# Values of the first chunk loaded ahead of the first weights, with shorter planned transfers, in a list-scheduled attention and mixture-of-experts kernel

## The chip, the cores and the metric

The kernel runs on one core of one Trainium2 chip. The metric is the device time of one execution in microseconds; a kernel's time is the median of its runs. All runs shown here are of the undisturbed ("fast") state. Engines are called PE (TensorE), ACT (ScalarE), DVE (VectorE), POOL (GpSimd) and SP (SyncE). PEld is PE's weight load.

## The reference

```python
# B, H, S, D = 4, 8, 768, 48: gated linear attention, one state per head
f = 1.0 / (1.0 + np.exp(-f_logit))
for t in range(S):
    state = f[:, :, t, :, None] * state + np.einsum('bhd,bhe->bhde', k[:, :, t], v[:, :, t])
    y[:, :, t] = np.einsum('bhd,bhde->bhe', q[:, :, t], state)
# x = y as (3072, 384); 4 experts of 384 -> 1024 -> 384, mixed by probabilities
p = domain_probs / (domain_probs.sum(-1, keepdims=True) + 1e-09)
for e in range(E):
    h = np.maximum(x @ w1[e], 0.0)
    out += p[:, e:e + 1] * (h @ w2[e])
```

## The kernel before

The sequence is cut into six chunks of 128 steps, with four batches each. Each step of the work (a load, an activation, a group of matmuls) is an `Op` with a cost on each engine that may run it, a priority and a lag until its result can be used. A planner places the ops on modelled engines. The instructions are then emitted in the planned order, and on the chip each engine runs its own in order. So a planned duration has no effect of its own on the chip. It decides which instruction stands before which.

```python
    def ready(self, o, e):
        t = 0.0
        for d in o.deps:
            if d.end is None:
                return None
            t = max(t, d.end + (d.lag + self.LATENCY if d.engine != e else 0.0 if e == "PE" else 0.05))
        return t
    ...
            for e in ("PE", "ACT", "DVE", "POOL", "DMA"):
                while free_at[e] <= now + 1e-9:
                    for o in left:            # sorted by priority: the first that is ready
```

Loads of q, k and f go out on SP's queue. Chunk 0's values, cast to bf16 on the way, and all expert weights go out on POOL's queue. An op on the modelled engine "DMA" stands for the transfer behind such an issue and emits nothing.

```python
    def add_load(c, nm, b, n, prio, deps=(), cost=None):
        op = P.add(f"ld {nm}{c}.{b}", {"DMA": cost or (1.05 if c else 1.1) * n}, ..., lag=2.0)
    v_gate, issued = [(0, "k", 1), (0, "k", 2)], []
    def add_v(b, prio):
        issued.append(P.add(f"v issue {b}", {"POOL": 0.8}, ..., -600 + b,
                            deps=issued[-1:] + ([ld[v_gate[b]]] if b < 2 else []), lag=1.2))
        ld[0, "v", b] = P.add(f"ld v0.{b}", {"DMA": 1.1}, lambda _: None, prio, deps=issued[-1:], lag=2.0)
    for i, x in enumerate("f0 k0 q0 f1 k1 q1 f2 f3 k2 q2 v0 k3 q3 v1 v2".split()):
        ...
    for i, (e, which, ks, cols) in enumerate(pieces):          # 11 weight pieces
        iss = P.add(f"w issue {i}", {"POOL": 0.8}, ..., -600 + 3 * i, deps=issued[-1:] + ...)
        op = P.add(f"w {i}", {"DMA": 2.05 if i < 6 else 4.4}, lambda _: None, ..., deps=[iss], lag=1.0)
        if i == 0:
            add_v(B - 1, -459.5)                               # v3 after the first weights
```

Weight pieces are numbered from 1 in this text. Pieces 1 and 2 are the halves of expert 0's first matrix, 3 and 4 those of expert 1's, 5 and 6 the halves of expert 0's second matrix; the other five are whole matrices. PE's part before the first expert matmul is padded with matmuls on a constant tile ("fillers", line L644 or L642), as many as the plan has gaps:

```python
    for o in done:
        if o.engine == "PE" and o.start <= first:
            o.pad, t = int((o.start - t) / (0.42 if t < 7.0 else 0.25)), o.end
```

L374 is the first expert matmul (x times w1, into h), L389 the second (h times w2, into o), L310 and L365 transposes, L325 the attention scores, L340 the scores times v, L301 the products of q and k with the gates, L246 weight issues, L233 value issues. An h group is three L374 matmuls, an o group four L389 (with piece 5 or with piece 6). In the views of waits, L385 is the relu of h on ACT, L396 the sum of o on DVE, L226 and L228 are copies.

Of the kernel before, what the change touches and what calls it, by code (L numbers as in the profile page):

```python
# [102 lines left out]
def kernel(  # L103
# [12 lines left out]
    B, H, S, D = q.shape  # L116
# [23 lines left out]
    P = Plan(rooms)  # L140
# [90 lines left out]
    def load(c, nm, b, n):  # L231
        if (c, nm) == (0, "v"):
            ins[c, nm, b] = nc.gpsimd.dma_start(out=tl("vb", c, b), in_=srcs[nm][c, :, b * H:(b + n) * H, :])  # L233
            if b < 2:
                after(ins[c, nm, b], ins[v_gate[b]])
            return
        ins[c, nm, b] = nc.sync.dma_start(out=tl(nm, c, b // 2)[:, hh(b, n), :],  # L237
                                          in_=srcs[nm][c, :, b * H:(b + n) * H, :])
        if (c, nm, b) == (1, "f", 0):
            after(ins[c, nm, b], ins["w", 6])  # L240
        if (c, nm, b) == (1, "f", 1):
            after(ins[c, nm, b], ins["w", w_gate])
# [162 lines left out]


    ld = {}
    def add_load(c, nm, b, n, prio, deps=(), cost=None):
        op = P.add(f"ld {nm}{c}.{b}", {"DMA": cost or (1.05 if c else 1.1) * n}, lambda e: load(c, nm, b, n), prio,
                   deps=deps, takes=[(nm, c, b // 2)], lag=2.0)  # L410
        for i in range(n):
            ld[c, nm, b + i] = op
        return op


    v_gate, issued = [(0, "k", 1), (0, "k", 2)], []

    def add_v(b, prio):
        issued.append(P.add(f"v issue {b}", {"POOL": 0.8}, lambda _: load(0, "v", b, 1), -600 + b,
                            deps=issued[-1:] + ([ld[v_gate[b]]] if b < 2 else []), takes=[("vb", 0, b)], lag=1.2))  # L420
        ld[0, "v", b] = P.add(f"ld v0.{b}", {"DMA": 1.1}, lambda _: None, prio, deps=issued[-1:], lag=2.0)

    for i, x in enumerate("f0 k0 q0 f1 k1 q1 f2 f3 k2 q2 v0 k3 q3 v1 v2".split()):
        nm, b = x[0], int(x[1])
        if nm == "v":
            add_v(b, -1000 + i)
        else:
            add_load(0, nm, b, 1, -1000 + i)

    every = slice(0, None)  # L430
    pieces = [(e, 1, every, slice(i * F // 2, (i + 1) * F // 2)) for e in range(2) for i in range(2)]
# [2 lines left out]
    w_last, w_gate = len(pieces) - 1, len(pieces) - 3  # L434
    wd = {}
    for i, (e, which, ks, cols) in enumerate(pieces):
        if i == 7:
            add_load(1, "f", 0, 1, -454.5, deps=wd[2, 1], cost=0.1)
        if i == w_last:
            for x in ((1, "f", 1, 1), (1, "k", 0, 2), (1, "q", 0, 2), (1, "v", 0, 2)):  # L440
                add_load(*x, -430 + len(ld), deps=wd[3, 1])
        iss = P.add(f"w issue {i}", {"POOL": 0.8}, lambda _, i=i, x=(e, which, ks, cols): load_w(i, *x),
                    -600 + 3 * i, deps=issued[-1:] + ([ld[1, "k", 0]] if i == w_last else []))
        op = P.add(f"w {i}", {"DMA": 2.05 if i < 6 else 4.4}, lambda _: None, -400 if i == w_last else -460 + i, deps=[iss], lag=1.0)
        issued.append(iss)
        wd[e, which] = wd.get((e, which), []) + [op]
        if i == 0:
            add_v(B - 1, -459.5)
    for x in ((1, "f", 2, 2), (1, "k", 2, 2), (1, "q", 2, 2), (1, "v", 2, 2)):
        add_load(*x, -400 + len(ld), deps=wd[3, 1])  # L450

# [3 lines left out]
    def attention(c, slot, gran):  # L455
        G, X, Y, GS, ET, VB = {}, [], [], [], {}, {}
        more = c < C - 1
        for b0 in range(0, B, gran):
            p, d, half = slot(b0, 0) - 0.5, 0.43 if gran == 1 else 0.84, b0 // 2
            g1 = P.add(f"gate1 {c}.{b0}", {"ACT": d}, lambda e, b0=b0: gate1(c, b0, gran), p,  # L460
                       deps=[ld[c, "f", b0 + i] for i in range(gran)], takes=[("ex", c, b0)], frees=[("f", c, half)])
            g2 = P.add(f"gate2 {c}.{b0}", {"ACT": d}, lambda e, b0=b0: gate2(c, b0, gran), p + 0.1,
                       deps=[g1], takes=[("gp", c, half)], frees=[("ex", c, b0)])
            for b in range(b0, b0 + gran):
                G[b] = g2
        for b in range(B):
            s = lambda k: slot(b, k)
            half = b // 2
            pt_ = lambda kind, *x: ("ps_t", kind, c, b) + x
            on = lambda f, *x: (lambda e, b=b: f(c, b, *x))  # L470
            one = lambda f, *x: (lambda e, b=b: f(c, b, *x, e))
            cs = P.add(f"cs {c}.{b}", {"PE": 0.17 if c else 0.36}, on(pe_cs), s(0),
                       deps=[G[b]], takes=[pt_("cs")], lag=0.2, frees=[("gp", c, half)])
            ex = P.add(f"exps {c}.{b}", {"ACT": 0.98 if c else 0.82}, on(exps), s(0) + 0.1, deps=[cs],
                       takes=[("e", c, b)] + ([("egs", c, b)] if c == 0 else []), frees=[pt_("cs")])
            GS.append(P.add(f"egs {c}.{b}", {"POOL": 0.8}, on(dma_egs), s(10), deps=[ex], takes=[("egs", c, b)],
                            frees=[("e", c, b)], lag=2.8) if c and more else None)
            pe = {"DVE": 0.47} if c == 0 and b == B - 1 else {"DVE": 0.47, "POOL": 1.36} if c == 0 else None
            qm = P.add(f"q {c}.{b}", pe or ({"DVE": 0.8} if (c, b) < (1, 2) else {"POOL": 1.1}), one(product, 0), s(4) - 0.2,
                       deps=[ex, ld[c, "q", b]], takes=[("qk", c, b)], frees=[("q", c, half), ("e", c, b)])  # L480
            km = P.add(f"k {c}.{b}", pe or ({"DVE": 0.5} if (c, b) < (1, 2) else {"POOL": 1.0}), one(product, 1), s(4) - 0.1,
                       deps=[ex, ld[c, "k", b]], takes=[("qk", c, b)], frees=[("k", c, half), ("e", c, b)])
            vb = ld[0, "v", b] if c == 0 else P.add(f"v {c}.{b}", {"POOL": 0.5, "ACT": 0.52} if c == 1 else {"POOL": 0.5}, one(cast_v), s(4),
                       deps=[ld[c, "v", b]], takes=[("vb", c, b)], frees=[("v", c, half)])
            if (c, b) < (1, 2):
                tq = P.add(f"tpq {c}.{b}", {"PE": 0.22}, on(pe_tp, 0), s(4), deps=[qm],
                           takes=[pt_("tp")], frees=[("qk", c, b)], lag=0.2)
                tk = P.add(f"tpk {c}.{b}", {"PE": 0.22}, on(pe_tp, 1), s(4) + 0.01, deps=[km],
                           takes=[pt_("tp")], frees=[("qk", c, b)], lag=0.2)
                parts = [(slice(0, 2), [tq, tk])] if c or b < B - 1 else [(slice(j, j + 1), [tj]) for j, tj in enumerate((tq, tk))]  # L490
                et = [P.add(f"ev_tp {c}.{b}", {"DVE": 0.69, "ACT": 1.05} if c else {"DVE": 0.6, "ACT": 0.92} if len(parts) == 1 else {"DVE": 0.35, "ACT": 0.49},
                            lambda e, b=b, js=js: copy(e, tl("QK", c, b)[0:MP, js], tl("tp", c, b)[0:MP, js]), s(4) + 0.1,
                            deps=ds, takes=[("QK", c, b)], frees=[pt_("tp")]) for js, ds in parts]
            else:
                et = [P.add(f"tp {c}.{b}", {"DMA": 1.8}, on(dma_tp), s(4), deps=[qm, km], takes=[("QK", c, b)],
                            frees=[("qk", c, b)], lag=2.5)]
            ET[b], VB[b] = et, vb
# [181 lines left out]
```

## Time and profile before

| kernel before | value |
|---|---|
| time, median (range of the first 3 runs) | 298.62 us (298.36 to 298.94) |
| profiled span | 296.6 us |
| PE busy | 289.0 us, 97% |
| PE idle after the first expert matmul, by its waits | 0.6 us |
| first expert matmul starts | 19.75 us |
| weight pieces 1, 2, 5, 6 land at | 19.10, 21.98, 27.74, 29.75 us |

A line of a timeline is: start, duration, engine, line, operation, output<-inputs, shapes, count, and in brackets how long the engine was idle before it and what ended that.

### The profile page before, as it was taken

The page shows a single profiled execution, that of the slowest core. Times are in us where ns is not written, and L with a number is a line of the kernel's source. Part 1 is how long each engine was busy: PE and PEld are TensorE (multiplying, and loading weights), DVE is VectorE, ACT ScalarE, POOL GpSimd, SP SyncE. Part 2 cuts the span into 40 slices and gives each one's busy share as a digit, 9 for nine tenths or more (in the row PEclk, how much of TensorE's full clock was granted, in tenths as well). Part 3 has the DMA queues.
Part 4 walks back from the last instruction along what each step waited for, and adds up shares of the span by engine and source line. Part 5 has one row for each costly group of instructions (what it writes and reads, how often), then busy time and mean ns, then how long its engine had stood idle before and what let it go on. Part 6 is the DMA issues. An engine that isn't in the chain of part 4 may idle for free.

```text
span 296.6 us, 5591 instructions
## 1 busy us (share of the span) xinstructions
PE 289.0 (97%) x2172; PEld 170.0 (57%) x2172; DVE 126.1 (43%) x250; ACT 174.3 (59%) x317; POOL 106.1 (36%) x180
## 2 busy tenths in 40 slices
PE   6899999999999999999999999999999999999995
PEld 2476555567777775555555555555555555555553
DVE  6786012785763673045375235243523222101223
ACT  5656656666684667777477575554475544465440
POOL 5786401138767448144449372243220000000000
PEclk9999999999999999999999999999999999999999
DMA  7999999998979999998979932102432100200002
GB/s 157 200 169 206 207 192 210 189 210 167 201 152 166 191 171 185 209 187 164 198 133 218 179 60 35 27 0 67 122 61 30 27 2 27 80 2 0 0 2 106
DMA packets 136462, 36.43 MB, mean 123 GB/s; under 512 B 126812, under 2 KB 135644, under 8 KB 136436
## 3 DMA queue, kind: packets, MB, share of 16 engines
q1 hardware_dynamic: 125188, 29.35, 52.0%
q0 software_dynamic: 11248, 6.72, 16.4%
q8 instruction: 17, 0.28, 0.4%
q14 instruction: 9, 0.07, 0.1%
HBM read 31.51 MB, written 4.72 MB: 122 GB/s over the span
## 4 chain that ended last, share of the span: by engine, by line
PE 78%; DMA 14%; POOL 3%; SPq 2%; issue 1%; ACT 1%; DVE 0%; POOLq 0%
PE ps_m L389 37%; PE ps_m L374 35%; DMA w_sb<-in_moe_w_dram 10%; DMA k<-in_k_dram 4%; SPq L237 2%; POOL w_sb L246 2%; PE ps_t L325 2%; PE ps_t L340 1%; PE ps_t L336 1%; PE ps_t L273 1%; POOL vb L233 1%; PE ps_t L346 1%; ACT e L293 1%; DVE o L396 0%; ACT xT L226 0%
## 5 line engine op out<-in xcount | busy, mean ns | idle before, releaser
L385 ACT ACTIVATE h<-ps_m 128x512 bf16<-128x512 f32 (+2 forms) x188 | 102.4, 548 | 91.9 <-PE ps_m L374 88.9
L374 PE MATMUL ps_m<-xT,w_sb 128*128 128x512 bf16 (+3 forms) x708 | 152.8, 339 | 0.6 <-ACT xT L226 0.6
L389 PE MATMUL ps_m<-w_sb,h 128*128 128x384 bf16 (+1 forms) x776 | 152.6, 324 | 0.1
L389 PEld LDWEIGHTS <-h 128*128 128x128 bf16 x776 | 75.0, 98 | 59.0 <-DMA w_sb<-in_moe_w_dram 0.3
L396 DVE SCALAR_TENSOR_TENSOR o<-ps_m,pn,o 128x384 f32<-128x384 f32 (+1 forms) x73 | 44.5, 612 | 117.3 <-PE ps_m L389 111.1
L374 PEld LDWEIGHTS <-w_sb 128*128 128x128 bf16 x708 | 65.3, 98 | 43.5 <-issue 0.7
L301 POOL TENSOR_TENSOR qk<-q,e 128x384 bf16<-128x384 f32 x18 | 21.4, 1195 | 36.5 <-ACT e L293 34.3
L360 POOL TENSOR_TENSOR Sf<-Sf,egs 48x192 f32<-48x192 f32 x40 | 20.2, 504 | 36.5 <-DVE Sf L353 34.4
L329 DVE TENSOR_TENSOR AT<-ps_t,mask 128x512 bf16<-128x512 f32 x48 | 30.2, 683 | 5.1 <-PE ps_t L325 5.1
L383 DVE TENSOR_SCALAR h<-ps_m 128x256 bf16<-128x256 f32 (+2 forms) x40 | 19.3, 499 | 26.5 <-PE ps_m L374 13.1
L293 ACT ACTIVATE e<-ps_t 128x384 f32<-128x384 f32 x48 | 26.7, 668 | 5.0 <-PE ps_t L273 3.5
L301 POOL TENSOR_TENSOR qk<-k,e 128x384 bf16<-128x384 f32 x20 | 20.2, 1013 | 8.7 <-ACT e L293 5.5
L353 DVE TENSOR_TENSOR Sf<-Sf,ps_t 48x192 f32<-48x192 f32 x40 | 14.0, 350 | 10.3 <-PE ps_t L346 9.4
L246 POOL DMA_DIRECT2D w_sb<-in_moe_w_dram x11 | 8.8, 807 | 18.5 <-DMA k<-in_k_dram 17.2
L361 POOL CAST sb<-Sf 48x192 bf16<-48x192 f32 x40 | 13.6, 340 | 2.6
L398 ACT ACTIVATE o<-ps_m,pn 128x384 f32<-128x384 f32 x22 | 12.8, 582 | 2.5 <-PE ps_m L389 1.5
L644 PE MATMUL ps_m<-busy 128*128 128x512 bf16 x34 | 10.9, 423 | 1.5 <-DVE busy L144 1.5
L265 ACT ACTIVATE ex<-f 128x768 f32<-128x768 f32 (+1 forms) x14 | 10.4, 746 | 1.8 <-DMA f<-in_f_logit_dram 1.8
L298 POOL DMA_DIRECT2D egs<-e x16 | 9.0, 563 | 6.9 <-ACT e L293 6.9
L340 PE MATMUL ps_t<-vb,AT 128*128 128x48 bf16 x192 | 11.4, 184 | 0.0
L269 ACT ACTIVATE gp<-ex 128x768 bf16<-128x768 f32 (+1 forms) x14 | 10.5, 751 | 0.3
L340 PEld LDWEIGHTS <-AT 128*128 128x128 bf16 x192 | 9.9, 97 | 1.1
(54 smaller groups left out, 120.6 us busy)
## 6 DMA issues: line engine op xcount, KB each, us to landing
out_dram<-o SPq DMA_DIRECT2D x23, 192.0 KB, 2.0
w_sb<-in_moe_w_dram POOLq DMA_DIRECT2D x5, 768.0 KB, 18.0
k<-in_k_dram SPq DMA_DIRECT2D x10, 384.0 KB, 5.6
q<-in_q_dram SPq DMA_DIRECT2D x10, 384.0 KB, 5.5
v<-in_v_dram SPq DMA_DIRECT2D x10, 384.0 KB, 5.7
f<-in_f_logit_dram SPq DMA_DIRECT2D x9, 384.0 KB, 4.6
w_sb<-in_moe_w_dram POOLq DMA_DIRECT2D x6, 384.0 KB, 9.0
f<-in_f_logit_dram SPq DMA_DIRECT2D x6, 192.0 KB, 3.8
```

The lines of the kernel that those rows point to most:

```text
L246: ins["w", i] = nc.gpsimd.dma_start(out=w[:, e, ks, cols], in_=r[e][:, ks, cols])
L293: nc.scalar.activation(out=o, in_=i, func=AF.Exp, scale=1.0 if j else -1.0)
L301: engines[eng].tensor_tensor(out=tl("qk", c, b)[:, j, :, 0:D].rearrange("t (i r) d -> t i r d", r=2), in0=tl("qk"[j], c, b // 2)[:, hh(b), ...
L329: nc.vector.tensor_tensor(out=tl("AT", c, b)[:, r].rearrange("s i t -> s (i t)"), in0=tl("A", c, b, r).rearrange("s i t -> s (i t)"), in1= ...
L340: nc.tensor.matmul(out=y[:, h * D:(h + 1) * D], lhsT=AT[:, r, i, :], rhs=vb[:, h, :], start=(c == 0), stop=True, skip_group_check=True)
L353: nc.vector.tensor_tensor(out=Sf[rows, b], in0=Sf[rows, b], in1=KV[rows, :, r, :], op=ALU.add)
L360: nc.gpsimd.tensor_tensor(out=Sf[rows, b], in0=Sf[rows, b], in1=eg, op=ALU.mult)
L374: nc.tensor.matmul(out=hp(c, e, fc, n0, n1, nf)[:, f], lhsT=w1_sb[:, e, kk, (fc + f) * 128:(fc + f + 1) * 128], rhs=tl("xT", c)[:, kk, n0: ...
L383: nc.vector.tensor_relu(out=dst, in_=src)
L385: nc.scalar.activation(out=dst, in_=src, func=AF.Relu)
L389: nc.tensor.matmul(out=tl("op", c, e, nt, part)[:, cols], lhsT=tl("h", c, e, half_of(c, nt * T))[:, fc, nt * T:(nt + 1) * T], rhs=w2_sb[:, ...
L396: nc.vector.scalar_tensor_tensor(out=o, in0=op, scalar=pe, in1=o, op0=ALU.mult, op1=ALU.add)
```

## The change

Its intent is to have the values of all four batches earlier, to let POOL make products of q and k instead of running through weight issues, and to start PE's expert stream earlier by a plan with shorter transfers.

```diff
-        op = P.add(f"ld {nm}{c}.{b}", {"DMA": cost or (1.05 if c else 1.1) * n}, ..., lag=2.0)
+        op = P.add(f"ld {nm}{c}.{b}", {"DMA": cost or (1.05 if c else 1.1) * n}, ..., lag=lag)
-    v_gate, issued = [(0, "k", 1), (0, "k", 2)], []
+    v_gate, issued = [(0, "k", 1), (0, "f", 3)], []
-        issued.append(P.add(f"v issue {b}", {"POOL": 0.8}, ...
-        ld[0, "v", b] = P.add(f"ld v0.{b}", {"DMA": 1.1}, ..., lag=2.0)
+        issued.append(P.add(f"v issue {b}", {"POOL": 0.95}, ...
+        ld[0, "v", b] = P.add(f"ld v0.{b}", {"DMA": 0.87}, ..., lag=1.4)
-    for i, x in enumerate("f0 k0 q0 f1 k1 q1 f2 f3 k2 q2 v0 k3 q3 v1 v2".split()):
+    for i, x in enumerate("f0 k0 q0 f1 k1 q1 f2 f3 k2 v0 q2 v1 k3 v2 q3 v3".split()):
-            add_load(0, nm, b, 1, -1000 + i)
+            add_load(0, nm, b, 1, -1000 + i, cost=0.87, lag=1.5)
-                    -600 + 3 * i, deps=issued[-1:] + ...
-        op = P.add(f"w {i}", {"DMA": 2.05 if i < 6 else 4.4}, ..., lag=1.0)
+                    (-600 if i == 0 else -185) + 3 * i, deps=issued[-1:] + ...
+        op = P.add(f"w {i}", {"DMA": 1.95 if i < 6 else 4.2}, ..., lag=1.0)
-        if i == 0:
-            add_v(B - 1, -459.5)
-            ex = P.add(f"exps {c}.{b}", {"ACT": 0.98 if c else 0.82}, ...
+            ex = P.add(f"exps {c}.{b}", {"ACT": 0.98 if c else 0.95}, ...
-            pe = {"DVE": 0.47} if c == 0 and b == B - 1 else {"DVE": 0.47, "POOL": 1.36} if c == 0 else None
+            pe = {"DVE": 0.5, "POOL": 1.15} if c == 0 else None
```

More of the change, by code (lines that the diff above doesn't have):

```diff
@@ L407, with add_load @@
     ld = {}
-    def add_load(c, nm, b, n, prio, deps=(), cost=None):
+    def add_load(c, nm, b, n, prio, deps=(), cost=None, lag=2.0):
         op = P.add(f"ld {nm}{c}.{b}", {"DMA": cost or (1.05 if c else 1.1) * n}, lambda e: load(c, nm, b, n), prio,
-                   deps=deps, takes=[(nm, c, b // 2)], lag=2.0)
+                   deps=deps, takes=[(nm, c, b // 2)], lag=lag)
         for i in range(n):
@@ L413, in add_load @@
         return op
-    v_gate, issued = [(0, "k", 1), (0, "k", 2)], []
+    v_gate, issued = [(0, "k", 1), (0, "f", 3)], []
     def add_v(b, prio):
-        issued.append(P.add(f"v issue {b}", {"POOL": 0.8}, lambda _: load(0, "v", b, 1), -600 + b,
+        issued.append(P.add(f"v issue {b}", {"POOL": 0.95}, lambda _: load(0, "v", b, 1), -600 + b,
                             deps=issued[-1:] + ([ld[v_gate[b]]] if b < 2 else []), takes=[("vb", 0, b)], lag=1.2))
-        ld[0, "v", b] = P.add(f"ld v0.{b}", {"DMA": 1.1}, lambda _: None, prio, deps=issued[-1:], lag=2.0)
-    for i, x in enumerate("f0 k0 q0 f1 k1 q1 f2 f3 k2 q2 v0 k3 q3 v1 v2".split()):
+        ld[0, "v", b] = P.add(f"ld v0.{b}", {"DMA": 0.87}, lambda _: None, prio, deps=issued[-1:], lag=1.4)
+    for i, x in enumerate("f0 k0 q0 f1 k1 q1 f2 f3 k2 v0 q2 v1 k3 v2 q3 v3".split()):
         nm, b = x[0], int(x[1])
@@ L442 @@
         iss = P.add(f"w issue {i}", {"POOL": 0.8}, lambda _, i=i, x=(e, which, ks, cols): load_w(i, *x),
-                    -600 + 3 * i, deps=issued[-1:] + ([ld[1, "k", 0]] if i == w_last else []))
-        op = P.add(f"w {i}", {"DMA": 2.05 if i < 6 else 4.4}, lambda _: None, -400 if i == w_last else -460 + i, deps=[iss], lag=1.0)
+                    (-600 if i == 0 else -185) + 3 * i, deps=issued[-1:] + ([ld[1, "k", 0]] if i == w_last else []))
+        op = P.add(f"w {i}", {"DMA": 1.95 if i < 6 else 4.2}, lambda _: None, -400 if i == w_last else -460 + i, deps=[iss], lag=1.0)
         issued.append(iss)
         wd[e, which] = wd.get((e, which), []) + [op]
-        if i == 0:
-            add_v(B - 1, -459.5)
     for x in ((1, "f", 2, 2), (1, "k", 2, 2), (1, "q", 2, 2), (1, "v", 2, 2)):
@@ L473, in attention @@
                        deps=[G[b]], takes=[pt_("cs")], lag=0.2, frees=[("gp", c, half)])
-            ex = P.add(f"exps {c}.{b}", {"ACT": 0.98 if c else 0.82}, on(exps), s(0) + 0.1, deps=[cs],
+            ex = P.add(f"exps {c}.{b}", {"ACT": 0.98 if c else 0.95}, on(exps), s(0) + 0.1, deps=[cs],
                        takes=[("e", c, b)] + ([("egs", c, b)] if c == 0 else []), frees=[pt_("cs")])
```

## The prediction

> **What bounds the kernel now.** I first read the page's chain of waits and its slices, then TensorE's waits after the start-up, then the timelines of PE and POOL in the first 25 us, then the DMA's own record.
>
> From the page of the kernel before (busy tenths in 40 slices of 7.4 us, and the chain that ended last):
> ```profile
> PE   6899999999999999999999999999999999999995
> DMA  7999999998979999998979932102432100200002
> ...
> PE 78%; DMA 14%; POOL 3%; SPq 2%; issue 1%; ACT 1%; DVE 0%; POOLq 0%
> ```
> PE is full from the third slice to the last one: the kernel is a PE stream with a start-up before it. The DMA engines are full as well for about the first 60 us.
>
> The waits of PE, from 19.5 us to the end, have one entry only:
> ```profile
> PE ps_m L374 <- ACT xT L226: 0.6, 1, 0.6
> ```
> So after 19.5 us the PE stream has 0.6 us of holes. The time is (start of the first useful expert matmul) + (a fixed amount of PE work) + (holes) + (tail). A change in the start-up can win only what it moves that start, or lose what holes it opens.
>
> The PE timeline where the stream starts (start, duration, what):
> ```profile
> 19.11 0.81 PE L644 MATMUL ps_m<-busy 128*128 128x512 bf16 x3
> 19.75 0.82 PE L374 MATMUL ps_m<-xT,w_sb 128*128 128x256 bf16 x6
> ```
> L644 is filler that computes nothing; L374 is the first expert matmul. Its start has two conditions: xT of batches 0 and 1 (ACT's copy for batch 1 runs from 19.10 to 19.58) and the first weight piece, which is issued at 13.16 and takes 5.9 us to land (19.10). They are 0.5 us apart, so neither can be moved alone for a gain of more than that.
>
> The chain that ended last, in order of time, from 20 to 60 us:
> ```profile
> 20.53 21.10 DMA w_sb<-in_moe_w_dram
> ...
> 42.07 7.75 DMA k<-in_k_dram
> ...
> 50.37 8.82 DMA w_sb<-in_moe_w_dram
> 59.19 0.05 issue
> 59.24 0.82 PE ps_m L389 x4
> ```
> Up to 59.24 the chain is a stream of transfers, and PE takes the last weights 0.05 us after they land. So there are two bounds with almost no slack between them, PE's work and the DMA stream. A PE that starts earlier meets the same weights at the same time, unless the stream moves too.
>
> POOL's timeline, which orders the software DMA queue:
> ```profile
> 6.31 1.00 POOL L301 TENSOR_TENSOR qk<-k,e 128x384 bf16<-128x384 f32 x1 [2.43 <-ACT egs L295]
> 7.64 1.06 POOL L233 DMA_DIRECT2D vb<-in_v_dram  x1 [0.33 <-DMA k<-in_k_dram]
> 8.89 1.24 POOL L301 TENSOR_TENSOR qk<-k,e 128x384 bf16<-128x384 f32 x1 [0.19 <-ACT egs L295]
> 11.35 1.83 POOL L233 DMA_DIRECT2D vb<-in_v_dram  x2 [1.21 <-DMA k<-in_k_dram]
> 13.16 0.76 POOL L246 DMA_DIRECT2D w_sb<-in_moe_w_dram  x1
> 13.89 0.93 POOL L233 DMA_DIRECT2D vb<-in_v_dram  x1
> 14.81 5.51 POOL L246 DMA_DIRECT2D w_sb<-in_moe_w_dram  x7
> ```
> The values v1 and v2 wait for k2 (landed 11.05), v3 stands behind the first weights, and from 14.81 POOL does nothing but weight issues, so the products of batches 2 and 3 all fall to DVE.
>
> **What the Trainium skill says.** "DMA: Bandwidth & Descriptors", section "Queues, rings and completion order": each engine takes packets in turn from the queues that have work. The trace agrees: the q load that shared the engines with v0 landed 2.2 us after the load before it, against 0.9 us for loads alone. The same page, "Anatomy of one DMA": a software-queue transfer has about 2 us fixed besides its bytes; here the v issued at 11.35 first shows traffic in the queue in the 13 to 14 us window, which agrees. "SBUF — State Buffer", section "SBUF: two separate sides": a DVE instruction with two SBUF inputs and a GpSimd one that reads SBUF exclude each other. The trace fits: POOL's product took 1.24 us with a DVE product beside it for 0.4 us and 1.00 us with almost none. So POOL is a poor place for a product, but it is free of the PSUM work that DVE alone carries.
>
> **The change, part by part.** The program has a planner that lists instructions by priority on modelled engines; the diff changes its costs and order. What the chip then does is set by in-order queues. I worked the first 16 us of the new plan by hand from the costs in the code.
>
> 1. *v1 gated on f3 instead of k2.* f3 lands at 10.10, k2 at 11.05. POOL sat idle 1.21 us before v1, so v1, v2 are issued about 0.95 us earlier (10.4 and 11.35), v3 at 12.3 (13.89 before, 1.6 us earlier), and the first weights at 13.2 (13.16 before): one issue of 0.93 us comes in front of them and 0.95 us is won by the gate. The sum is about zero.
>
> 2. *v3 ahead of the first weights in the queue.* Its packets took about 0.8 us (the software queue moved 1264 packets in the 14 to 15 us window; a v has 128 x 8 = 1024). If the queue is saturated, the first weights land 0.8 us later, 19.9. But between 15 and 18 us the queue moved only 0.41 MB, against 0.2 MB per us later, so about 1 us is slack there; then they land near 19.1 as before. I take 19.0 to 20.0.
>
> 3. *Values move in among q2, k3, q3.* k3 and q3 share the engines with v1 and v2: estimated one to two transfers of 0.8 us later, q3 at 16.2 to 17.2 instead of 15.35.
>
> 4. *Weights 1 and later rank behind POOL's products.* In my hand plan DVE now does q1 and k1, and POOL does k2 and then q3 after the first weight issue. DVE loses two products (2 x 0.55 us) of batches 2 and 3 and gains k1. On the chip POOL then waits for q3: 16.2 to 17.2, plus 1.15 us, so weight issue 1 is at 17.4 to 18.4 instead of 14.81. The queue needs it by about 17 (first piece done near 18.5 to 19, less 2 us fixed). So the stream may starve by 0 to 1.5 us, less the slack that part 2 used: pieces 1 to 5 shift by -0.5 to +0.8 us.
>
> 5. *xT of batches 0 and 1.* In the old order y1 (17.45) stood behind transposes that waited for late copies. v1 lands about 1.4 us earlier and k1 is done 0.3 us earlier, so y1 could run near 15.9 and xT near 17.6. But in my plan the transposes of q3 stand before the transpose of batch 1; if POOL makes q3 at 17.4 to 18.4, xT comes at 18.5 to 19.6. Against 19.58, that is a gain of 0 to 1 us.
>
> 6. *Shorter planned loads.* These give fewer fillers (L644) and an earlier planned start (my plan: first weights at 18.1, while about 19.4 is to be expected). Fillers that vanish become idle, which costs nothing unless PE cools; it still has attention work in between.
>
> Sum: the start is max(xT 18.5 to 19.6, weights 19.0 to 20.0) plus 0.15 us, near 19.4, against 19.75: -0.35 us. The DMA stream to 59 us carries the same bytes and shifts by about -0.5 to +0.8. As both bounds count, I expect between -1 and +1 us, centre -0.4: 298.62 - 0.4 = 298.2 us.
>
> **Rivals.** *The DMA stream as the only bound:* the chain up to 59.24 speaks for it, and the full DMA slices; then the new start is worth nothing and a starved queue shows in full: 299 to 300 us. Against it: most pieces have some tenths of us of slack at their first use. *Start-up latency as the only bound, weights keeping up:* xT at 18.5, start at 18.7, about 297.5 us. For it: 0.5 us between the two conditions, and 15 to 18 us is badly used; against it: v3 before the weights. *A reshuffled plan:* an earlier planned start moves priorities for later chunks and can remove or add holes such as the 0.6 us one at 67.38; about 0.5 us either way. *PE cools:* a wait of 2 us or more before the first weights; half-rate matmuls cost perhaps 1 us. The mean clock of 0.998 speaks against it, and the attention matmuls go on.
>
> **Range and chances.** The outcomes lie between 296.8 (both bounds 1.5 us earlier, with the hole gone) and 300.0 (the queue starved and PE waiting). Two per cent is 6.0 us; the whole start-up before 19.75 us is the only thing touched, and a third of it would have to vanish, or a hole of that size to open behind it. I give 0.01 to faster, 0.975 to same, 0.015 to slower.
>
> **What would show it.** POOL's timeline: four v issues ahead of the first weight issue, at about 10.4, 11.4, 12.3 for v1 to v3, the first weights at about 13.2, then one or two products before the second weights at 17.4 to 18.4. PE's timeline: first L374 near 19.4, fewer L644. The landing of the first weights: 19.0 to 20.0. PE's waits after the start: whether a wait on weights appears between 22 and 60 us. I would be wrong if POOL did not stop for q3 (then the weights come earlier and the gain is over 1 us), or if the new plan left PE waiting on weights that it believed to be there 1.3 us earlier.

## More of the kernel before

```profile
24.90 3.44 PE L374 MATMUL ps_m<-xT,w_sb 128*128 128x128 bf16 x33
28.18 1.46 PE L389 MATMUL ps_m<-w_sb,h 128*128 128x384 bf16 x8
29.48 0.81 PE L374 MATMUL ps_m<-xT,w_sb 128*128 128x512 bf16 x3
30.13 1.46 PE L389 MATMUL ps_m<-w_sb,h 128*128 128x384 bf16 x8
```

There is no bracket, so PE waits for nothing. The first L389 needs piece 5 at 28.18 and has had it since 27.74, when it landed; piece 6 landed at 29.75.

## The result, and the profile after

The changed kernel took 301.26 us (300.86 to 301.63, 4 runs) against 298.49 us for the kernel before in the same rounds. The ratio is 1.0088, 95% interval 1.0070 to 1.0105. Ratios here are the mean time of one kernel's fast runs over that of the other's of the same rounds, so not quite the ratio of the quoted medians. A repeat (r3) gave 1.0115 (1.0094 to 1.0136). The change costs about 2.7 us, where I had predicted a gain of 0.4 us and no more than 300.0 us.

The page of the changed kernel, slices and chain:

```profile
PE   6979999999999999999999999999999999999995
DMA  8999999998979879996989632102331100200002
...
PE 83%; DMA 7%; SPq 3%; POOL 3%; issue 1%; DVE 1%; ACT 0%; POOLq 0%; DVEq 0%; ACTq 0%
```

At this scale nothing is to be seen: PE looks as full as before. POOL's timeline is as predicted, with the four value issues ahead of the first weights, then two products, then the second weight issue, 2.2 us later than before:

```profile
10.22 2.64 POOL L233 DMA_DIRECT2D vb<-in_v_dram  x3 [1.66 <-DMA f<-in_f_logit_dram]
12.83 0.77 POOL L246 DMA_DIRECT2D w_sb<-in_moe_w_dram  x1
13.59 1.39 POOL L301 TENSOR_TENSOR qk<-k,e 128x384 bf16<-128x384 f32 x1
16.08 0.99 POOL L301 TENSOR_TENSOR qk<-q,e 128x384 bf16<-128x384 f32 x1 [1.10 <-DMA q<-in_q_dram]
17.01 7.17 POOL L246 DMA_DIRECT2D w_sb<-in_moe_w_dram  x9
```

The first piece lands at 19.18 and PE's stream starts at 19.23, so the start-up is where I had put it. The difference is in PE's waits from 18 us to the end, of which the kernel before had one, of 0.6 us:

```profile
PE ps_m L389 <- DMA w_sb<-in_moe_w_dram: 1.4, 2, 1.2
PE ps_m L374 <- ACT h L385: 0.4, 1, 0.4
PE ps_t L365 <- ACT yb L226: 0.3, 1, 0.3
PE ps_m L389 <- DVE o L396: 0.2, 1, 0.2
```

(Columns: who waited <- for whom: us in total, times, the longest.) The two waits on weights lie here, to be read against the four lines of the kernel before:

```profile
24.64 3.13 PE L374 MATMUL ps_m<-xT,w_sb 128*128 128x384 bf16 x32
27.99 0.82 PE L389 MATMUL ps_m<-w_sb,h 128*128 128x384 bf16 x4 [0.22 <-DMA w_sb<-in_moe_w_dram]
28.65 0.81 PE L374 MATMUL ps_m<-xT,w_sb 128*128 128x512 bf16 x3
30.64 0.81 PE L389 MATMUL ps_m<-w_sb,h 128*128 128x384 bf16 x4 [1.18 <-DMA w_sb<-in_moe_w_dram]
```

Two things differ. The work between is shorter: one h group of expert 1 before the first L389, where the kernel before has three; then one o group, one h group and at once the o group that needs piece 6, where the kernel before has two o groups on each side (the counts of 8). And piece 6 lands at 30.60, not 29.75. The chain of waits of the changed kernel leads from there back to POOL's product:

```profile
10.09 5.85 DMA q<-in_q_dram
...
16.08 0.99 POOL qk L301
17.07 3.07 POOL w_sb L246 x4
20.14 10.45 DMA w_sb<-in_moe_w_dram
30.60 0.04 issue
30.64 0.81 PE ps_m L389 x4
```

The traffic between 18 and 20 us shows what the late issue did, before first and changed below (for all queues: packets, bytes, mean rate, and how many packets were small):

```profile
DMA packets 1171, 0.36 MB, mean 179 GB/s; under 512 B 921, under 2 KB 1170, under 8 KB 1170
```
```profile
DMA packets 158, 0.16 MB, mean 79 GB/s; under 512 B 3, under 2 KB 158, under 8 KB 158
```

The queue ran nearly dry. Summed from 8 us on, the changed kernel has moved 0.17 MB less by 30 us, which is 0.8 us at the stream's 0.21 MB per us.

**A ledger of PE.** Some matmul records are missing from each trace, but the weight loads are complete: 2168 in the trace of the kernel before and 2157 in that of the changed one, in the order of the program (the four float32 transposes of the probabilities left out). I took the distance from each weight load to the next and subtracted the streaming time of its matmul, columns / 2.4 + 2.5 ns. The Trainium skill, "TensorE: Matmul & The Clock Gate", section "Back-to-back issue gap", gives this formula for an isolated matmul, and for a stream with weight loads about 131 ns at 512 columns. The trace has 216 ns for 512 columns with their weight loads, so the formula is what fits here and the 131 ns is not. What is left, summed by stretch, is loss. The start of the stream is that of the first L374 weight load, 19.54 in the kernel before. As differences to the kernel before, in us:

| stretch | changed | e4 | n3 | s1 | s2 | s3 |
|---|---|---|---|---|---|---|
| start of the expert stream | -0.31 | +1.17 | +0.05 | +0.36 | +0.80 | +0.09 |
| attention work left after the start | +0.36 | +0.36 | 0 | 0 | 0 | 0 |
| loss, start to 26 us | +0.67 | +0.20 | -0.12 | -0.12 | 0 | 0 |
| loss, 26 to 35 us (pieces 5 and 6) | +1.74 | +1.28 | 0 | +1.40 | -0.05 | +2.56 |
| loss, 35 to 54 us | 0 | +0.10 | +0.05 | +0.10 | +0.21 | 0 |
| loss, 54 to 70 us | -0.95 | -1.00 | -1.00 | -1.00 | -1.11 | -0.95 |
| loss, 70 to 90 us | +1.22 | +0.06 | +0.04 | +0.15 | +0.18 | +0.06 |
| after 90 us, and the tail | -0.06 | -0.08 | 0 | +0.34 | 0 | -0.06 |
| sum = difference of the profiled spans | +2.67 | +2.10 | -0.98 | +1.23 | +0.01 | +1.70 |

(The other columns are experiments below, one profile each. Sums can be off by 0.02 from rounding.) The largest entry of the changed kernel is the 1.74 us at pieces 5 and 6.

### The profile page after: what moved, and what is told of

Read it like the earlier page. It is cut to its first block, busy times and chain, and to the rows that moved or that the text cites. A ratio compares the mean times of both kernels' runs of the same rounds, so it can differ in the third digit from the quotient of the medians.

```text
span 299.2 us, 5540 instructions
## 1 busy us (share of the span) xinstructions
PE 287.7 (96%) x2133; PEld 169.8 (57%) x2161; DVE 127.4 (43%) x249; ACT 172.3 (58%) x316; POOL 107.8 (36%) x182
## 4 chain that ended last, share of the span: by engine, by line
PE 83%; DMA 7%; SPq 3%; POOL 3%; issue 1%; DVE 1%; ACT 0%; POOLq 0%; DVEq 0%; ACTq 0%
PE ps_m L389 40%; PE ps_m L374 37%; DMA w_sb<-in_moe_w_dram 3%; SPq L237 3%; DMA q<-in_q_dram 2%; PE ps_t L325 2%; POOL qk L301 1%; DMA egs<-e 1%; PE ps_t L340 1%; PE ps_t L336 1%; POOL w_sb L246 1%; PE ps_t L273 1%; PE ps_t L346 1%; DVE o L396 1%; DVE Sf L353 0%
## 5 line engine op out<-in xcount | busy, mean ns | idle before, releaser
L389 PE MATMUL ps_m<-w_sb,h 128*128 128x384 bf16 (+1 forms) x776 | 153.6, 324 | 1.8 <-DMA w_sb<-in_moe_w_dram 1.4
L374 PE MATMUL ps_m<-xT,w_sb 128*128 128x512 bf16 (+3 forms) x682 | 152.2, 338 | 1.7 <-ACT h L385 0.4
L389 PEld LDWEIGHTS <-h 128*128 128x128 bf16 x776 | 74.7, 98 | 61.4 <-issue 1.8
L374 PEld LDWEIGHTS <-w_sb 128*128 128x128 bf16 x708 | 65.5, 98 | 42.9 <-issue 0.8
L329 DVE TENSOR_TENSOR AT<-ps_t,mask 128x512 bf16<-128x512 f32 x48 | 29.9, 683 | 8.4 <-PE ps_t L325 8.4
L301 POOL TENSOR_TENSOR qk<-q,e 128x384 bf16<-128x384 f32 x19 | 22.4, 1184 | 25.7 <-ACT e L293 16.4
L383 DVE TENSOR_SCALAR h<-ps_m 128x256 bf16<-128x256 f32 (+1 forms) x41 | 20.5, 514 | 17.1 <-PE ps_m L374 15.1
L228 POOL CAST vb<-v 128x384 bf16<-128x384 f32 x17 | 8.4, 516 | 16.7 <-DMA v<-in_v_dram 12.3
L269 ACT ACTIVATE gp<-ex 128x768 bf16<-128x768 f32 (+1 forms) x14 | 10.4, 749 | 0.3
L226 ACT CAST yb<-ps_t 128x384 bf16<-128x384 f32 (+1 forms) x16 | 7.5, 471 | 5.1 <-PE ps_t L340 5.1
```

What stands on the lines that cost most here:

```text
L301: engines[eng].tensor_tensor(out=tl("qk", c, b)[:, j, :, 0:D].rearrange("t (i r) d -> t i r d", r=2), in0=tl("qk"[j], c, b // 2)[:, hh(b), ...
L329: nc.vector.tensor_tensor(out=tl("AT", c, b)[:, r].rearrange("s i t -> s (i t)"), in0=tl("A", c, b, r).rearrange("s i t -> s (i t)"), in1= ...
L374: nc.tensor.matmul(out=hp(c, e, fc, n0, n1, nf)[:, f], lhsT=w1_sb[:, e, kk, (fc + f) * 128:(fc + f + 1) * 128], rhs=tl("xT", c)[:, kk, n0: ...
L383: nc.vector.tensor_relu(out=dst, in_=src)
L389: nc.tensor.matmul(out=tl("op", c, e, nt, part)[:, cols], lhsT=tl("h", c, e, half_of(c, nt * T))[:, fc, nt * T:(nt + 1) * T], rhs=w2_sb[:, ...
```

## The experiments

**Theory B, the plan's order.** The planner's own dates for the landings of pieces 5 and 6 are 30.05 and 32.10 in the kernel before, which is 2.3 us later than they came (27.74, 29.75). In the changed kernel they are 25.87 and 27.82, which is 2.1 and 2.8 us earlier than they came (27.94, 30.60). The plan therefore puts the o groups too early, and an in-order PE stands before them with h groups behind that could run. **Theory A, the starved queue.** Products on POOL ahead of the second weight issue let the queue run dry, so all later pieces are late. **Rivals**: the values ahead of the weights, the new ranking of weight issues, or TensorE's clock.

Each call of runs shared one chip and the runs of the kernel before; calls went to different chips, so I compare ratios across calls.

### First call: one part undone, or one part alone

e1, the ranking of weight issues undone in the changed kernel:

```diff
-                    (-600 if i == 0 else -185) + 3 * i, ...
+                    -600 + 3 * i, ...
```

> The changed kernel with one part undone: weight issues rank ahead of POOL's products again, so the second weight issue follows the first product on POOL (about 15.0 us instead of 17.0). Theory A, the starved queue: in the changed kernel the stream moved 0.16 MB between 18 and 20 us against 0.36 MB before and stays 0.15 MB (0.75 us) behind; if the issue is earlier, the sixth weight piece lands near 29.8 instead of 30.6 and PE's wait for it (1.2 us) shrinks to about 0.4: about 300.2 us, and 299 if the starvation accounts for all of the loss. Theory B, the plan's order: the planner still believes that pieces 5 and 6 land at 25.9 and 27.8, so PE still asks for them too early: waits of 0.8 to 1.5 us stay, 300.5 to 301.3 us.

Measured: 301.01 us, ratio 1.0074 (1.0050 to 1.0097). Pieces now land earlier (21.50 for piece 2, 29.20 for piece 6), and no wait on pieces 5 and 6 is left in its profile. But the time hardly moved: the expert stream started at 20.57 us instead of 19.23. The mean clock, 0.994 in this profile, does not explain it: the four runs at 0.993 and 0.994 took 299.95 to 301.43 us, the two at 0.998 and 1.000 took 300.19 and 301.38.

e2, the planned landing of the weights 2 us later in the changed kernel:

```diff
-        op = P.add(f"w {i}", {"DMA": 1.95 if i < 6 else 4.2}, ..., lag=1.0)
+        op = P.add(f"w {i}", {"DMA": 1.95 if i < 6 else 4.2}, ..., lag=3.0)
```

> The changed kernel with one number changed: the planner believes that each weight piece lands 2 us later (planned landing of pieces 5 and 6: 27.9 and 29.8; seen in the changed kernel: 27.9 and 30.6). POOL's order is the same, so the queue starves as before. Theory B, the plan's order: PE's waits on the weights between 26 and 35 us (1.7 us lost) fall under 0.5 us: 299.3 to 300.0 us. Theory A, the starved queue: the weights are as late as before and PE only waits elsewhere: 301.0 to 301.4 us.

Measured: 299.55 us (299.11 to 301.55), ratio 1.0050 (1.0022 to 1.0078). e3, both edits:

> Both edits at once. If starved queue and plan's order each carry part of the loss: 298.3 to 299.2 us, the waits on weights gone and the sixth piece near 29.8. If a third cause carries it (the 1.2 us lost between 70 and 90 us, or the late attention of batches 2 and 3): 299.5 us or more with the waits gone.

Measured: 299.19 us (298.01 to 301.21), ratio 1.0026 (0.9993 to 1.0060).

The runs of e2 and e3 fall apart by their mean granted clock. In e2, four runs with 0.994 to 1.000 took 299.11 to 299.57 us and two with 0.989 took 301.10 and 301.55. In e3, three with 0.999 or more took 298.01 to 298.36, two with 0.994 took 300.03 and 300.17, and one with 0.989 took 301.21. The page's clock row in the changed kernel and in e2 (tenths, 40 slices):

```profile
PEclk9999999999999999999999999999999999999999
```
```profile
PEclk9969999999999999999999999999999999999999
```

And the fillers, two in the changed kernel, then four in e2:

```profile
18.18 0.59 PE L642 MATMUL ps_m<-busy 128*128 128x512 bf16 x2
```
```profile
21.82 1.88 PE L642 MATMUL ps_m<-busy 128*128 128x512 bf16 x4
```

In e2 they follow one another at 0.4 us, in the changed kernel at 0.22. The Trainium skill, "TensorE: Matmul & The Clock Gate", section "What's actually happening", has a gate that halves the clock after an idle window of some 3.4 us, and calls the window free-running. That agrees with the factor of two, and with runs of one kernel falling either way; no run here shows the window itself. So these experiments mix two things, and I read the runs that kept their clock: 299.1 to 299.6 for e2, 298.0 to 298.4 for e3. They were chosen after the fact, and not by one bound (a run at 0.994 counts in e2 and not in e3), so this is a hint and not a measurement of the two edits.

e4, the kernel before with only the planned transfers (0.87 and lags 1.5 and 1.4 for loads and values, 1.95 and 4.2 for weights, 0.95 for a value issue):

> The kernel before with nothing but the shorter planned transfers (loads 0.87, weights 1.95 and 4.2 us); values and priorities as before, weights issued one after another. Theory B, the plan's order: pieces 5 and 6 are planned at 26.8 and 28.8 and come near 27.8 and 29.8, so waits on weights appear that the kernel before does not have: 299.5 to 300.5 us. Theory A, the starved queue: no starvation here, so 298.0 to 298.7 us as before.

Measured: 300.02 us, ratio 1.0046 (1.0025 to 1.0068), where Theory B had it, in part by luck: by the ledger 1.28 us of the loss is at pieces 5 and 6, but 1.17 us is a later start, which no theory had. The waits on weights that the kernel before does not have appear with the planned numbers alone:

```profile
PE ps_m L389 <- DMA w_sb<-in_moe_w_dram: 0.9, 2, 0.7
PE ps_m L374 <- DVE xT L228: 0.5, 1, 0.5
```

It is not quite free of Theory A: the new plan also moved a product ahead of the first weight issue, which came at 14.52 instead of 13.16, so piece 1 landed at 20.67 and piece 6 at 31.85.

The new ranking on top of the kernel before needs no run: the orders of instructions on all engines come out the same as without it.

### Second call: the same with the clock held up

To take the clock out I added 14 fillers in the start-up to the changed kernel, e1, e2 and e3 alike:

```diff
-            o.pad, t = int((o.start - t) / (0.42 if t < 7.0 else 0.25)), o.end
+            o.pad, t = int((o.start - t) / (0.42 if t < 7.0 else 0.25)) + WARM.get(o.name, 0), o.end
+WARM = {"cs 0.0": 2, "y 0.1": 2, "tpk 0.3": 3, "tpq 0.3": 3, "xt 0.1": 2, "at 0.3": 2}
```

> The changed kernel with 14 more fillers in the start-up, so that TensorE's clock does not drop (some runs of the last experiments had filler spacing of 0.43 us between 17 and 23 us, twice the 0.22 of a warm clock, and were 1 to 3 us longer). The changed kernel itself had no such dip after 10 us, so nothing should change: 300.9 to 301.5 us, first expert matmul at 19.2 to 19.6, waits on weights as in the changed kernel. If the late warm-up (10 us instead of 5) were the cause of the loss: 299 us.

Measured: 301.59 us, ratio 1.0098 (1.0064 to 1.0132). One of its six runs had a lower clock (0.994, 304.07 us).

> The same fillers, and weight issues ranked ahead of POOL's products again. Without the clock dips of its first version this shows the starved queue alone: the second piece is issued near 15.0, pieces land 0.7 to 1.4 us earlier (sixth near 29.2), and the wait on them shrinks by about as much. Theory A: 299.7 to 300.4 us. If only the plan's order counts: 300.9 to 301.4 us.

Measured: 301.98 us, ratio 1.0088 (1.0057 to 1.0119), a miss. Its waits on pieces 5 and 6 are gone, but the ledger finds the losses of 70 to 90 us as in the changed kernel and a new hole of 1.4 us that ends at 116.5 us, where PE waits for a gate of ACT.

> The same fillers, and the planner told that weights land 2 us later; POOL's order as in the changed kernel. Theory B: like the undisturbed runs of its first version (299.1 to 299.6 us), now in all runs, with the waits on weights between 26 and 35 us gone and the loss between 70 and 90 us gone too. If the gain of those runs had another origin: above 300.5 us.

Measured: 299.57 us (299.33 to 300.60), ratio 1.0014 (0.9988 to 1.0040).

> The same fillers and both edits. If the two causes add up and the clock explains the spread of its first version (298.0 to 301.2 us): 298.0 to 298.5 us in all runs, mean clock 0.998 or more. If the clock has nothing to do with the spread, it stays 298 to 301.

Measured: 300.26 us (299.39 to 300.40), ratio 1.0032 (1.0006 to 1.0057), with clocks of 0.998 or more; the expected time was missed by 1 to 2 us.

The fillers did their work on the clock: the mean clock of 23 of the 24 runs is 0.998 or more. They did not bring the first warm-up forward (w1's fillers at 8.7 us still follow one another at 0.4 us, as the changed kernel's do), so the late warm-up that w1's expectation names was not tested; the changed kernel's stream starts early in spite of it. But the stream of w3 and w4 started at 22.2 and 22.5 us. How much of that the fillers did and how much the weights that were planned later is not told apart; with the fillers alone (w1) it started at 20.25. What stands is w3 against w1: the same order on POOL, the weights planned 2 us later, and 0.8% less time. Undoing the ranking alone (e1, w2) did not repair anything in either form.

### Third call: the values' order alone, and other plans

n1, the kernel before with only the new order of the values (gate, list, and v3 ahead of the first weights):

> The kernel before with the values' order alone (v1 gated on f3, v3 ahead of the first weights, values in among q2, k3, q3), old planned costs, old priorities. Weight issues follow one another right after v3, so the queue does not starve; the plan stays pessimistic (pieces 5 and 6 planned at 30.05 and 32.1, expected near 27.5 and 29.5), so no waits on weights. If the shorter planned loads are what costs 2.7 us: 298.0 to 299.2 us. If the values ahead of the weights are what costs: 300.5 to 301.5 us, with the first weights landing late.

Measured: 297.85 us, ratio 0.9970 (0.9952 to 0.9989). The values ahead of the weights are not the cause; they help.

n2, the changed kernel with the planned transfers put back:

```diff
-            add_load(0, nm, b, 1, -1000 + i, cost=0.87, lag=1.5)
+            add_load(0, nm, b, 1, -1000 + i)
-        ld[0, "v", b] = P.add(..., {"DMA": 0.87}, ..., lag=1.4)
+        ld[0, "v", b] = P.add(..., {"DMA": 1.1}, ..., lag=2.0)
-        op = P.add(f"w {i}", {"DMA": 1.95 if i < 6 else 4.2}, ...
+        op = P.add(f"w {i}", {"DMA": 2.05 if i < 6 else 4.4}, ...
```

> The changed kernel with the planned transfers (loads, values, weights) put back to the old durations and lags; order of values, new ranking of weight issues and new costs of products stay. The plan then puts no product ahead of the second weight issue, the same with the old ranking, so the ranking does nothing. If the planned durations are the cause, through both the early order and the products in front of the weight issue: 298.0 to 299.2 us, no waits on weights. If the ranking or the new product costs are the cause: above 300.5.

Measured: 298.38 us, ratio 0.9984 (0.9967 to 1.0002). With the old durations the whole loss is gone, although ranking and product costs are those of the change. The planned durations are the cause.

n3, the changed kernel with planned transfers near the measured ones, and the old ranking (with these durations the new ranking gives the same instructions in the same order):

```diff
-            add_load(0, nm, b, 1, -1000 + i, cost=0.87, lag=1.5)
+            add_load(0, nm, b, 1, -1000 + i, cost=0.9 if i < 9 else 1.1, lag=2.0)
-        ld[0, "v", b] = P.add(..., {"DMA": 0.87}, ..., lag=1.4)
+        ld[0, "v", b] = P.add(..., {"DMA": 0.9}, ..., lag=1.8)
-        op = P.add(f"w {i}", {"DMA": 1.95 if i < 6 else 4.2}, ..., lag=1.0)
+        op = P.add(f"w {i}", {"DMA": 1.95 if i < 6 else 4.2}, ..., lag=2.2)
```

> The changed kernel with planned transfers set to what the trace showed: loads 0.9 us each (1.1 for those beside the values) landing 2.2 us after, weights landing 2.4 us after (pieces 1, 2, 5, 6 planned at 19.9, 22.8, 28.6, 30.6). One product (k3) stays ahead of the second weight issue. If a plan that knows the real landings is what matters: no wait on weights over 0.3 us and 297.8 to 299.0 us. If an early start is bought with clock dips: runs spread to 301 with mean clocks of 0.99.

Measured: 297.52 us (296.95 to 297.89), ratio 0.9951 (0.9935 to 0.9968), with clocks of 0.998 to 1.000. It beats both kernels. (Its dates for pieces 5 and 6, 28.6 and 30.55, are still 1.4 and 0.8 us later than they came.) Its only wait of PE after the start, and the same place in PE's timeline:

```profile
PE ps_m L374 <- DMA w_sb<-in_moe_w_dram: 0.3, 1, 0.3
```
```profile
24.34 3.93 PE L374 MATMUL ps_m<-xT,w_sb 128*128 128x384 bf16 x36
28.11 1.46 PE L389 MATMUL ps_m<-w_sb,h 128*128 128x384 bf16 x8
29.41 0.81 PE L374 MATMUL ps_m<-xT,w_sb 128*128 128x512 bf16 x3
30.06 1.46 PE L389 MATMUL ps_m<-w_sb,h 128*128 128x384 bf16 x8
```

The groups of 8 are back: three h groups of expert 1 come before the first L389 and PE waits for nothing, although piece 6 landed at 29.72. n4, the same with weights planned 1.3 us later still:

> The same with weights planned 1.3 us later still (pieces 5 and 6 at 29.9 and 31.85), as far on the late side as the kernel before was. If erring late is harmless and erring early is what costs: 298.0 to 299.2 us, like the one planned as measured. If both directions cost: 299.5 or more.

Measured: 297.98 us, ratio 0.9972 (0.9954 to 0.9989). Erring late by 2.3 and 2.0 us on pieces 5 and 6 (planned at 29.9 and 31.85, landed at 27.57 and 29.84) costs 0.2% against n3, and the kernel is still ahead of the one before.

### Fourth call: the two effects apart

On the quiet n3 the two theories can be made by hand, the second less cleanly than the first. s1 lies about pieces 5 and 6 only; POOL's order is the same and PE gets the changed kernel's order of h and o groups at these pieces:

```diff
-        op = P.add(f"w {i}", ..., lag=2.2)
+        op = P.add(f"w {i}", ..., lag=-1.3 if i in (4, 5) else 2.2)
```

> The kernel planned as measured (297.5 us) with one lie: weight pieces 5 and 6 are planned 3.5 us earlier, at 25.1 and 27.05. POOL's and the start-up's order stay; PE now gets the order of the changed kernel, with one expert matmul group ahead of the first product with piece 5 and two ahead of that with piece 6, instead of three and four. If the order alone costs: PE reaches piece 6's product near 28.5 and the piece lands near 29.5, a wait of 0.8 to 1.3 us, and the time is longer by as much: 298.3 to 298.9 us. If the order is harmless without the starved queue: 297.3 to 297.8.

Measured: 299.14 us, ratio 1.0011 (0.9996 to 1.0025), 0.6% above n3's 0.9951. Its waits:

```profile
PE ps_m L389 <- DMA w_sb<-in_moe_w_dram: 1.1, 2, 0.8
PE ps_m L374 <- DMA w_sb<-in_moe_w_dram: 0.3, 1, 0.3
PE ps_m L374 <- ACT h L385: 0.2, 1, 0.2
```

s2 forces the q product of batch 3 onto POOL ahead of the second weight issue:

```diff
-            qm = P.add(f"q {c}.{b}", pe or (...
+            qm = P.add(f"q {c}.{b}", ({"POOL": 1.15} if (c, b) == (0, 3) else pe) or (...
-                    -600 + 3 * i, ...
+                    (-600 if i == 0 else -185) + 3 * i, ...
```

> The kernel planned as measured with the q product of batch 3 forced on POOL ahead of the second weight issue (as in the changed kernel: issue near 17 to 17.5 instead of 15.2), PE's order as planned as measured. If the starved queue alone costs: the stream falls 0.5 to 0.8 us behind, pieces land by as much later, and the time is longer by as much: 298.0 to 298.4 us. If PE's order has the slack for it: 297.3 to 297.8.

Measured: 298.79 us, ratio 0.9997 (0.9982 to 1.0012). Its traffic from 18 to 20 us:

```profile
DMA packets 292, 0.29 MB, mean 146 GB/s; under 512 B 6, under 2 KB 292, under 8 KB 292
```

n3 moved 0.40 MB there. But the edit did more than I expected of it. In this plan two h groups of expert 1, not three, stand before the first L389, and the order of the start-up differs from n3's as well. And PE's only wait in the profile is not at pieces 5 and 6:

```profile
PE ps_m L374 <- DMA w_sb<-in_moe_w_dram: 1.2, 1, 1.2
20.34 1.16 PE L374 MATMUL ps_m<-xT,w_sb 128*128 128x256 bf16 x9 [1.19 <-DMA w_sb<-in_moe_w_dram]
```

It is for piece 1, which was issued at 13.55, ahead of the forced product, and landed at 20.29 (n3: 13.03 and 19.55). So 0.75 of the 1.0 us between the two profiles lies in the start of the stream, with transfers that stand ahead of the second weight issue in the queue. Piece 5 landed at 28.19 (n3: 27.23), 0.14 us before PE asked for it, so an earlier start would have met a wait there. s3, both:

> Both at once. The wait for piece 6 should then be the sum of the two, 1.6 to 2.0 us, and the time 299.2 to 299.7 us if the two add up; that leaves 1 us or more of the changed kernel's 301.3 to its late attention of batches 2 and 3 and other order. If they overlap, 298.5 to 299.0.

Measured: 299.94 us, ratio 1.0039 (1.0024 to 1.0054). Its waits:

```profile
PE ps_m L389 <- DMA w_sb<-in_moe_w_dram: 2.2, 2, 1.2
```

### Fifth call: repeats on one chip

> The kernel planned as measured again, on one chip with the two runs below: if its lead of 0.5 per cent over the kernel before is real and not the chip's, 0.994 to 0.997 of the kernel before.

Measured: n3 again 297.33 us, ratio 0.9964 (0.9950 to 0.9979).

> The starved queue alone again, beside the planned as measured one. If it costs by itself: 0.3 to 0.5 per cent above that one (0.9 to 1.4 us). If the difference of the last run was that of the two chips: within 0.15 per cent of it.

Measured: s2 again 298.47 us, ratio 1.0000 (0.9985 to 1.0015), so 0.36% or 1.1 us above n3 on the same chip. The edit costs by itself. How much of this is the dry queue is not shown: by the ledger r2 is 0.9 us behind r1, 0.36 us of it in the start (piece 1 issued at 13.47, in r1 at 13.10) and 0.34 us at pieces 5 and 6, where PE waits 0.2 us for piece 5, landed at 28.24 (r1: 27.18).

> The changed kernel itself, on the same chip: 1.007 to 1.011 of the kernel before, so 1.2 to 1.5 per cent above the one planned as measured.

Measured: the changed kernel again 301.54 us, ratio 1.0115 (1.0094 to 1.0136), so 1.5% above n3 on the same chip. The wait is there again: piece 6 landed at 30.68, and the ledger has 1.74 us more than the kernel before between 26 and 35 us.

**What follows.** Against n3 (0.9951 and 0.9964), the early order costs 0.47 to 0.60%, the forced product 0.33 to 0.49% (four differences, the pair on one chip 0.36%), both 0.75 to 0.88%, which is close to their sum: 2.2 to 2.6 us. For the early order there is a second clean pair: s3 and s2 ran on one chip and have the same orders on POOL and DVE and the same fillers, and 0.42% lies between them. The share of the dry queue in the forced product's cost stays open. The changed kernel is another 0.5 to 0.8% (1.5 to 2.3 us) above s3. The ledger shows where this lies in the one profile: 1.0 us in attention of batches 2 and 3 that comes after the start of the stream and holds it up, and 1.2 us in holes between 76 and 86 us, which are there in the changed kernel, e1, w1, w2 and r3 and in no kernel with another plan. Both are gone with the old durations (n2). But the new durations on the old order (e4) do not make the holes of 76 to 86 us, and planning the weights alone 2 us later (e2, e3, w3, w4) removes them. Which order of which instructions makes them was not taken apart and stays open.

## Why the prediction was wrong

- **What bounds the kernel**: right. The time is the start of the stream, a fixed amount of work, and holes; the change lost by holes. I also wrote that PE and the DMA stream are two bounds with almost no slack between them, which is what bit.
- **Parts 1 to 3, transfers**: v1 to v3 were issued at 10.22, 11.10 and 11.97 (predicted 10.4, 11.35, 12.3), the first weights at 12.83 (13.2), landing at 19.18 (19.0 to 20.0). q3 landed at 15.94, a little earlier than the 16.2 to 17.2 that I gave it. Right in kind and nearly in size. One reading was loose: the 2 us that I set beside the v issue at 11.35 lie before its first packet, while the page that I named puts most of the fixed 2 us after the last byte. The trace agrees with the size and not with the place.
- **Part 4, POOL**: k2 and q3 went to POOL ahead of the second weight issue, which came at 17.01 (17.4 to 18.4 predicted). Pieces 1 to 5 landed between 0.01 us earlier and 0.20 us later than in the kernel before, inside my -0.5 to +0.8, but piece 6 was 0.85 us late, and pieces 7 to 10 as much. Of the 0.85 us, 0.65 is a longer time from piece 5 to piece 6 (2.66 us against 2.01), which has no cause here (see the last list). The right measure is not the kernel before but n3, with the same values ahead and no dry queue: its piece 5 landed at 27.23, 0.7 us before the changed kernel's. So the late issue ate what the new order of values had won at piece 5. That the queue would run dry was foreseen rightly. The size was not: my sum counted it as near zero, and s2 and r2 put 1.0 to 1.5 us on the edit that makes it, of which the dry queue's own share is not shown.
- **Part 5, the start**: 19.23 us against about 19.4. Right. It was worth nothing by itself: the attention work that was left behind it (+0.36 us) and the losses up to 26 us (+0.67 us) ate the 0.31 us.
- **Part 6, the shorter planned loads**: this is the step that failed. I asked what they do to the fillers and to the planned start, and stopped there; the range was even drawn from "the whole start-up before 19.75 us is the only thing touched". The same durations carry through the whole plan, and set where the first uses of pieces 5 and 6 stand in PE's order. I worked the plan by hand for the first 16 us and read "1.3 us earlier" at the first weights; at pieces 5 and 6 the gap was 2.1 and 2.8 us. The runs put 1.4 to 1.8 us on this order alone (s1), and 1.74 us in the changed kernel's ledger with the late queue.
- **The rivals**: "most pieces have some tenths of us of slack at their first use" was read from the old order, and the change replaced that order. The last line, on what would make me wrong, names the right cause, "PE waiting on weights that it believed to be there 1.3 us earlier", but no part of the range was given to it. A range up to 300.0 had no room for a plan that errs.
- **The clock**: nothing in the changed kernel's profile after 10 us, as predicted, but the experiments e2 and e3 show that a start-up can fall into it, at 1 to 3 us. The number of fillers does not decide this: e2's program has 28, as n3's, and the changed kernel's 23, and these two kept their clock.
- **The intent of the change** was good in one part. With the values' order alone (n1) the kernel is 0.3% faster, and with durations as measured (n3) 0.4 to 0.5%. Even there the gain is not in the start-up: the ledger has n3's stream starting where it did before, and the gain is the 1.0 us between 54 and 70 us, the hole at 67.4 us of the kernel before among it.

## What to carry to other kernels

Where a planner fixes the order for in-order engines, its durations are part of the kernel: dates that are too early make an engine wait in front of data with other work behind it, while dates that were 2 us too late cost 0.2% here, against dates that were 1 us too late. So compare each planned landing with the trace before shortening it, and err late. And look at what an issue on a compute engine's queue stands behind: a second product in front of the second weight issue, and the plan that came with it, cost 0.3 to 0.5% here, while one product there (n3) did not keep that kernel from being the fastest.

## What the Trainium skill lacked or had wrong

- "DMA: Bandwidth & Descriptors", "Anatomy of one DMA", gives 2.0 us + bytes / 436 GB/s. For the transfers here that cast from float32 to bf16, the rate fits if the bytes are those read: a 384 KB piece, which reads twice as much (0.79 MB, an estimate of 1.8 us), followed the one before at 1.9 us. Even then the sum is short for a piece issued to a nearly dry queue: piece 2 of the changed kernel took 5.0 us from issue to landing, where 2.0 + 0.79 MB / 0.436 gives an estimate of 3.8 us.
- "TensorE: Matmul & The Clock Gate", section "What's actually happening", says for modelling that the ramp penalty is under 1% of a typical span. That figure is of one ramp. Where the clock dropped once more within the start-up (the fillers of e3's profile follow one another at 0.22 us at 12.1 us and at 0.43 us at 19.6 us), the cost came to as much again: in e3 the runs with a mean clock of 0.999 or more took 298.0 to 298.4 us and the one with 0.989 took 301.2 us, 1.0% more.
- No page says what an early planned date costs an in-order engine against a late one: 0.5 to 0.6% where two pieces were planned 2.4 and 2.8 us before they landed (s1 against n3), 0.2% where they were planned 2.3 and 2.0 us after (n4 against n3, whose own dates were 1.4 and 0.8 us late).
- No page has a cause for this: piece 6 landed 1.9 to 2.0 us after piece 5 in the kernel before, e3, n1, n2, s2 and r2, and 2.3 to 3.1 us after it in n3, n4, s1, s3, r1, r3 and the changed kernel, for the same 384 KB. The DMA engines kept their rate meanwhile (0.43 MB in the 2.01 us of the kernel before, 0.57 MB in the 2.66 us of the changed one), so a slower queue is not the reason. Part of the wait for piece 6 is this. It stays open.
